# Packed attention with a routed feed-forward: copy of the turned pairs, order of the upper half and the route, start of batch 1

## Chip, cores and metric

One core of a Trainium2 chip runs the kernel. The metric is device time in microseconds (us) of one execution, lower is better. Engines are named as in the profile: PE (TensorE), DVE (VectorE), ACT (ScalarE), POOL (GpSimd), SP (SyncE, which issues DMAs).

## What is computed

Two stages on 8 batches. In the first, 32 pack queries `p` gather each head's keys and values, and the 576 queries attend to the 32 packed rows. In the second, each of the 4608 tokens goes through the one of eight experts whose embedding is nearest.

```python
def _attn_ref(q, k, v, p):                  # q, k, v: 8 x 8 x 576 x 64, p: 8 x 8 x 32 x 64
    p_packed = sm_attn(p, k, v)             # softmax(p k^T / 8) v
    return sm_attn(q, p_packed, p_packed)   # softmax(q pp^T / 8) pp

def _moe_ref(x, expert_emb, tau, w1, w2):   # x: 4608 x 512, w1: 8 x 512 x 1024
    logits = xn @ en.T / tau                # rows of x and emb divided by their norms
    expert_idx = np.argmax(logits, axis=1)
    gate_w = softmax(logits)[arange, expert_idx]
    for e in range(E):
        h = np.maximum(x[mask] @ w1[e], 0.0)
        out[mask] = gate_w[mask, None] * (h @ w2[e])
```

## The kernel before

The tokens of a batch mostly go to one expert. The kernel guesses it for the whole batch (`guess`), loads that expert's weights, runs the feed-forward of all 576 tokens with it, and counts afterwards how many tokens chose another; a loop behind the main one repeats a batch where there are any.

Most products are made of three passes, high by high, high by low and low by high: a value is cast on ACT to the high part and the rest is formed by a subtraction on DVE or POOL.

**What a batch's attention does, in order.** `att1`: the keys' scores (`key_scores`), their softmax; `pack`: the packed values land in one PSUM tile for two groups of heads (`values`); DVE multiplies them by the reciprocal sums and by masks, once for pairs of rows (`pair_rows`, tile `pp2`), once for four rows (`quad_rows`, L400, tile `pp`, 128x256, one instruction for each of two head groups); PE turns the pairs into the bank `pu` (`pair_turn`), a copy brings that into `T` (L496), and four products of `T` with the embeddings give the packed rows' logits (`row_logits`, L431). `rows_split` casts the four rows' products on ACT (L277) and subtracts on POOL (L278), into `ppx`. Then come the queries' scores against `T` (`query_scores`, L263, 16 products in two halves of 288 tokens) and the guess (L544 with a few small DVE steps, and a register load for the weights' DMAs).

`att2`: the softmax of the queries' scores in two halves, 0 and 1, each: transpose from PSUM (`unpack`, L586), `biggest` (L591), `shift` (L597), exponential on ACT (L600), `total` (L606), `norm` (L612), transpose back (`turn`, L621), and its split into `AT`: `high` a cast on ACT (L627), `low` a subtraction on DVE (L631). Then `route`: five tiles of up to 128 tokens. Each has six products of `AT` with `ppx` (L683), which give the logits' sums and the tokens' outputs; DVE reduces the logits (L692), and ACT squares the outputs with a running sum (L699) for the norm. Tiles 0 and 1 need half 0 of `AT` alone, the third tile (c = 2, tokens 256 to 383) is the first that needs half 1; its first products need the high part, the third the low. Two PSUM buffers `pt` hold the tiles: the third stands in the buffer of the first, the fourth in that of the second, and each is free when its reduction and its square are done. The square's output is of no use; it is written to a scratch tile with the tag `at`, of which there is one buffer, the same that the turned half lies in until `low` has read it.

Behind the route come the one-hot and the `counts` (L717, L727), and the `gates` (a chain of 128x5 steps, L106 to L111 and L744 onwards, a part of it on POOL in batch 0, then the spreading of the tail's gates, 16 small copies on ACT, L773).

**The feed-forward**, `ffn`: folding the packed values into the first weights (L836 to L850), 16 hidden products per half (L918, with a relu on ACT at L920 and the rest on DVE at L921), then the tail tokens, four tiles of 24 products of 320 columns (L946; `turn_tail`, L1266, transposes each tile on DVE while the next one's products run), then the output tiles, 24 products of 512 columns each (L964; the store's scaling at L1248).

**What sets the order.** Everything is issued in the order in which Python runs it. `ffn` yields after every few products; at each yield one step (sometimes two) of the next batch's attention is issued, so the attention of batch b+1 lies in batch b's feed-forward. `idle(n)` lets n such steps pass with nothing, and `alternate` takes one step of each of two generators by turns, the first named first. An engine executes its own instructions in that order and waits where an operand or a buffer isn't ready. For batch 0 a string, `PLAN`, says step by step what is issued beside the feed-forward: `a` is a step of batch 1's attention, `k` a flip of its queries, `r` a step of batch 0's route, `g` of its gates, `s` of its softmax. `tight` and `early` in the code mean batch 1, `first` and `fine` batch 0.

## Time and profile before

| | us |
|---|---|
| time, median of 3 runs | 460.75 (460.24 to 460.81) |
| the profiled execution | 461.09 |
| its span, first to last instruction | 459.5 |
| PE busy in the span | 430.4 (94%) |
| DVE / ACT / POOL busy | 316.0 / 217.8 / 148.2 |
| batch 2's feed-forward, start to start of batch 3's | 52.96 (148.30 to 201.26) |
| PE busy in it | 51.02 |
| PE busy between 56 and 70 (batch 0's feed-forward) | 10.13 of 14.00 |
| mean granted clock of PE | 0.993 of full speed |

The table's first half says that PE works nearly all the time and DVE two thirds of it. Batches 1 to 3 pass at the same pace, 52.94 to 52.96 each, so one of them stands for the middle of the run; the first one, in which batch 1's attention has to be started beside batch 0's, is different, and PE is idle there for almost 4 us in one stretch of 14. A share of busy time does not say who decides: for that one follows the waits and, from the end backwards, the chain of releases.

### The profile page before, as it was taken

Reading aid. Unit: us, or ns where it says so; the run is one execution under the profiler, and the core shown is the slowest. Engines: PE = TensorE matmul, PEld = TensorE weight load, DVE = VectorE, ACT = ScalarE, POOL = GpSimd, SP = SyncE. Lnnn points to the kernel's source line nnn. Section 1 sums busy time; section 2 is a strip of 40 time slices with the busy share of each in tenths; the row PEclk is TensorE's granted clock in tenths of the full one; section 3 lists DMA queues with packets and bytes.
Section 4 is the critical chain, followed back from the end, with each engine's and each line's share of the span. In section 5 each row is a group of like instructions: output and inputs, shape, how many; then the busy total and the mean of one; then the engine's idle time right before and its main releaser. Section 6 shows DMA issues by size and latency. Waiting matters only on the chain.

```text
span 459.5 us, 10722 instructions
## 1 busy us (share of the span) xinstructions
PE 430.4 (94%) x3890; PEld 364.9 (79%) x3891; DVE 316.0 (69%) x957; ACT 217.8 (47%) x580; POOL 148.2 (32%) x199
## 2 busy tenths in 40 slices
PE   8799979999999999999999999999999999899993
PEld 6547769788986979779887879869887888779993
DVE  5468869568974789648985689748895589535420
ACT  2456633675435733366443734357433754337300
POOL 2446564153403513053402524044221524026000
PEclk9999998999999999999999999999999999999998
DMA  7989899648995589854997479955798403621022
GB/s 208 293 271 260 232 262 316 181 97 212 300 317 130 133 228 328 235 123 124 255 350 174 100 211 304 296 110 134 234 359 209 108 3 122 245 57 47 3 59 51
DMA packets 48860, 88.23 MB, mean 192 GB/s; under 512 B 11992, under 2 KB 30488, under 8 KB 48800
## 3 DMA queue, kind: packets, MB, share of 16 engines
q1 hardware_dynamic: 40512, 57.96, 48.6%
q0 software_dynamic: 8000, 29.43, 18.0%
q8 instruction: 32, 0.52, 0.5%
q14 instruction: 28, 0.23, 0.2%
q10 hardware_dynamic: 288, 0.08, 0.1%
HBM read 78.00 MB, written 9.44 MB: 190 GB/s over the span
## 4 chain that ended last, share of the span: by engine, by line
PE 58%; DVE 27%; ACT 4%; DMA 4%; issue 3%; POOL 1%; SPq 1%; DVEq 0%; ACTq 0%; POOLq 0%
PE pf L964 19%; PE pf L918 17%; PE pf L946 5%; PE pt L683 4%; PE pt L836 3%; DVE hT L921 3%; DVE st L586 2%; PE pt L388 2%; DVE at L621 2%; DVE st L597 2%; PE pt L263 2%; DVE s L606 2%; DVE st L612 2%; DVE pp L400 2%; DVE mx L591 2%
## 5 line engine op out<-in xcount | busy, mean ns | idle before, releaser
L812 POOL TENSOR_TENSOR w2s<-w2r,w2s 128x512 fp32r<-128x512 f32 x61 | 78.5, 1292 | 168.9 <-ACT w2s L811 168.9
L946 PE MATMUL pf<-hT,w2s 128*128 128x320 f32 x768 | 124.3, 313 | 0.0
L946 PEld LDWEIGHTS pf<-hT,w2s 128*128 128x128 f32 x768 | 114.8, 190 | 3.7 <-issue 3.3
L918 PE MATMUL pf<-AT,G 128*128 128x288 f32 x720 | 103.7, 298 | 0.1
L918 PEld LDWEIGHTS pf<-AT,G 128*128 128x128 f32 x720 | 97.3, 188 | 4.7 <-issue 2.3
L964 PE MATMUL pf<-w2s,hT 128*128 128x512 f32 (+1 forms) x408 | 94.1, 383 | 0.0
L964 PEld LDWEIGHTS pf<-w2s,hT 128*128 128x128 f32 x408 | 72.0, 188 | 20.0 <-issue 5.9
L921 DVE SCALAR_TENSOR_TENSOR hT<-pf,hT 128x288 fp32r<-128x288 f32 x128 | 56.4, 446 | 20.2 <-ACT hT L920 20.2
L920 ACT ACTIVATE hT<-pf 128x288 fp32r<-128x288 f32 x128 | 51.4, 414 | 38.8 <-PE pf L918 37.5
L811 ACT CAST w2s<-w2r 128x512 fp32r<-128x512 f32 x64 | 39.0, 626 | 28.2 <-issue 26.4
L683 PE MATMUL pt<-ppx,AT 128*128 128x264 f32 (+1 forms) x240 | 38.3, 291 | 7.9 <-ACT at L699 6.8
L683 PEld LDWEIGHTS pt<-ppx,AT 128*128 128x128 f32 (+1 forms) x240 | 32.3, 177 | 12.5 <-ACT at L699 8.6
L850 DVE TENSOR_TENSOR G<-pt,G 128x512 fp32r<-128x512 f32 x28 | 19.4, 691 | 30.3 <-ACT G L849 30.3
L699 ACT ACTIVATE at<-pt 128x512 f32<-128x512 f32 (+1 forms) x40 | 23.9, 597 | 30.6 <-DVE lg L692 30.5
L278 POOL TENSOR_TENSOR ppx<-pp,ppx 128x256 fp32r<-128x256 f32 x16 | 11.4, 734 | 44.8 <-ACT ppx L277 44.8
L773 ACT COPY gt<-gate 32x2 f32<-32x2 f32 (+1 forms) x128 | 24.6, 192 | 2.2 <-DVE hit L1237 0.7
L600 ACT ACTIVATE st<-st 128x576 f32<-128x576 f32 (+1 forms) x17 | 11.2, 658 | 29.1 <-issue 19.5
L627 ACT CAST AT<-at 128x576 fp32r<-128x576 f32 x16 | 10.8, 673 | 27.8 <-DVE at L621 27.8
L849 ACT CAST G<-pt 128x512 fp32r<-128x512 f32 x28 | 16.5, 588 | 15.1 <-DVE G L850 12.0
L1266 DVE STREAM_TRANSPOSE ot<-pf 128x320 f32<-128x320 f32 x32 | 16.2, 506 | 9.9 <-PE pf L946 9.5
L293 DVE STREAM_TRANSPOSE kt<-nat 128x576 f32<-128x576 f32 x28 | 21.4, 764 | 0.1
L795 POOL DMA_DIRECT2D w2r<-in_moe_w x28 | 19.8, 713 | 0.0
(183 smaller groups left out, 491.8 us busy)
## 6 DMA issues: line engine op xcount, KB each, us to landing
nat<-in_k SPq DMA_DIRECT2D x112, 140.0 KB, 3.2
nat<-in_q SPq DMA_DIRECT2D x112, 140.0 KB, 3.8
w1t<-in_moe_w POOLq DMA_DIRECT2D x14, 1024.0 KB, 7.4
w2r<-in_moe_w POOLq DMA_DIRECT2D x28, 512.0 KB, 10.1
nat<-in_v SPq DMA_DIRECT2D x32, 160.0 KB, 3.8
out<-ot SPq DMA_DIRECT2D x28, 160.0 KB, 3.1
nat<-in_v SPq DMA_DIRECT2D x32, 128.0 KB, 4.0
out<-o SPq DMA_DIRECT2D x60, 64.0 KB, 1.7
```

Source lines behind the costliest of these rows:

```text
L293: nc.vector.transpose(kt.rearrange("p (n i) -> p n i", i=32), t)
L683: nc.tensor.matmul(pt[:r, 512 * g : 512 * g + XW], AT[:, a, g, c * P : c * P + r], x.ppx[:, m, g], start=(i == 0), stop=(i == 2),)
L699: nc.scalar.activation(scr[:r, :, : HB * D], ptv[:r, :, 0 : HB * D], AF.Square, accum_out=ss[:r, c : c + 1])
L773: copy(dst[32 * a : 32 * a + 32, k : k + HB * (n - 1) + 1 : HB], src[32 * k : 32 * k + 32, NCT : NCT + n],)
L795: queue.dma_start(t, w2e[:, 2 * i : 2 * i + 2, :])
L811: nc.scalar.copy(hi, raw)
L812: eng.tensor_tensor(out=lo, in0=raw, in1=hi.bitcast(F32), op=ALU.subtract)
L918: nc.tensor.matmul(pf[:, :HS], w, r, start=(n == 0), stop=(n == len(ops) - 1))
L920: nc.scalar.activation(hT[:, 0, f, cs], pf[:, :HS], AF.Relu)
L921: nc.vector.scalar_tensor_tensor(out=hT[:, 1, f, cs], in0=pf[:, :HS], scalar=0.0, in1=hT[:, 0, f, cs].bitcast(F32), op0=ALU.max, op1=ALU.s ...
L946: nc.tensor.matmul(pf[:, : S - TL], x.w2s[f][:, m, mt * P : mt * P + P], hT[:, a, f, TL:], start=(n == 0), stop=(n == len(ops) - 1),)
L964: nc.tensor.matmul(pf[:, :w], hT[:, a, f, c * P : (c + 1) * P], x.w2s[f][:, m, at : at + w], start=(f == 0 and i == 0), stop=(f == NF - 1 ...
```

## The change

It consists of these parts.

- In `pack`, for batches 2 to 7, the copy of `T` is issued ahead of the four rows' products. For batch 1 the copy moves from DVE to ACT.
- In `route`, the square's scratch tile takes the tag `st` (two buffers, those of the halves' scores) in place of `at`, but not in batch 0.
- In `softmax`, the cast and the subtraction of half 1 (`high(1)`, `low(1)`) are issued behind the first route tile's reduction and square. Three idle steps stand ahead of the route and two ahead of its second tile, and the alternation with the next keys begins with the keys.
- For batch 1 (`early`) both halves are unpacked first, the guess is issued ahead of the query scores, the query flips may start after the key scores, `shift` of half 1 is on DVE instead of POOL, and the rows of `PLAN` change to match; batch 0's route and counts come in other steps.

```diff
@@ -485,18 +485,20 @@
             if not tight:
                 yield
             pu = ps.tile([P, 512], F32, name="pu", tag="pf")
-            for g in range(NG):
-                quad_rows(x, g, pts[g])
             if tight:
+                for g in range(NG):
+                    quad_rows(x, g, pts[g])
                 yield
             for g in range(NG):
                 pair_turn(x, g, pu)
             if not tight:
                 yield
-            nc.vector.tensor_copy(x.T, pu[:, 0 : NG * P])
+            (nc.scalar.copy if tight else nc.vector.tensor_copy)(x.T, pu[:, 0 : NG * P])
             if tight:
                 yield
             else:
+                for g in range(NG):
+                    quad_rows(x, g, pts[g])
                 for g in range(NG):
                     rows_split(x, g)
                 yield from idle(2)
@@ -511,6 +513,8 @@
                 logits_split(x)
 
         key_scores(x)
+        if tight:
+            x.queries = queries()
         yield
         if tight:
             for g in range(NG):
@@ -520,7 +524,6 @@
                 key_exp(x, g)
                 key_sum(x, g)
                 yield
-            x.queries = queries()
             yield from pack()
             return
         for g in range(NG):
@@ -638,6 +641,8 @@
                 (unpack, 0), (biggest, 0), (shift, 0), (unpack, 1), (biggest, 1), (total, 0),
                 (shift, 1), (norm, 0), (turn, 0), (total, 1), (low, 0), (norm, 1), (turn, 1),
             )
+            if early:
+                order = (order[0], order[3], order[1], order[2], *order[4:])
             if first:
                 names = dict(
                     U=unpack, B=biggest, S=shift, X=expo, T=total, N=norm, R=turn, H=high, L=low
@@ -648,19 +653,23 @@
                 step(hf, *gs)
                 if step is shift and not first:
                     expo(hf)
-                if step is turn and not first:
+                if step is turn and not first and not hf:
                     high(hf)
                 yield
             if first:
                 return
-            yield
-            low(1)
             if not after:
+                high(1)
+                low(1)
                 return
-            yield
+            yield from idle(3)
             steps = route(x)
             yield next(steps)
-            yield from alternate(steps, after)
+            next(steps)
+            high(1)
+            low(1)
+            yield from idle(2)
+            yield from alternate(after, steps)
 
         yield from softmax()
 
@@ -673,6 +682,7 @@
         x.routed = lg, ss
 
     def route(x, fine=False):
+        scratch = dict(name="at", tag="at") if fine else dict(name="st", tag="st", bufs=2)
         AT = x.AT
         lg, ss = x.routed
         for c in range(NC5):
@@ -695,7 +705,7 @@
                 axis=AX.X,
                 op=ALU.add,
             )
-            scr = sb.tile([P, NG, HS], F32, name="at", tag="at")
+            scr = sb.tile([P, NG, HS], F32, **scratch)
             nc.scalar.activation(
                 scr[:r, :, : HB * D], ptv[:r, :, 0 : HB * D], AF.Square, accum_out=ss[:r, c : c + 1]
             )
@@ -1035,10 +1045,13 @@
                 counts(bat[b - 1])
             yield from att1(x, nat_main(b), b == 1)
             if b == 1:
+                expert = guess(x)
+                next(expert)
                 query_scores(x)
                 yield
-            expert = guess(x)
-            next(expert)
+            if b > 1:
+                expert = guess(x)
+                next(expert)
         second = att2(x, keys_main(b + 1) if b else None, b == 0, b == 1)
         if b == 1:
             drain(expert)
@@ -1301,13 +1314,13 @@
 
     PLAN = (
         "qssq", "sssssssss", "sss", "ss", "ss", "ssG", "", "sG", "ssa", "ssa",
-        "a", "sa", "a", "GG", "w", "aq", "aq", "a", "aq", "qw",
-        "aW", "wWa", "Wr", "wk", "rrak", "akw", "rka", "a", "a", "a",
-        "ra", "arr", "rra", "ra", "rra", "ra", "ga", "ga", "ga", "ga",
+        "a", "sa", "a", "GG", "w", "aq", "aq", "a", "aq", "qwk",
+        "aW", "wWa", "Wr", "wk", "rrak", "arkw", "a", "a", "a", "a",
+        "ra", "rra", "rra", "ra", "a", "a", "ga", "ga", "ga", "rrga",
         "ga", "a", "aag", "ga", "ga", "ga", "g", "g", "gaa", "a",
         "aa", "a", "a", "a", "g", "", "", "", "", "",
     )
-    POOLED = ("S1",)
+    POOLED = ()
     DBL = 8
     LAG = 2
```

DVE in batch 3's feed-forward, around the copy of `T` for batch 4 (`pp` are the four rows' products, `hT` the relu's rest, `rq_t` and `gy` steps of the gates). Before:

```order
L921 SCALAR_TENSOR_TENSOR hT<-pf,hT 128x288
L400 SCALAR_TENSOR_TENSOR pp_4017<-pt,ri,mask_77 128x256
L400 SCALAR_TENSOR_TENSOR pp_4019<-pt,ri,mask_77 128x256
L106 TENSOR_TENSOR rq_t<-rq_h,gy 128x5
L108 TENSOR_TENSOR rq_t<-rq_t,gy 128x5
L111 SCALAR_TENSOR_TENSOR gy<-rq_t,gy 128x5
L921 SCALAR_TENSOR_TENSOR hT<-pf,hT 128x288
L496 COPY T<-pu 128x256
L744 TENSOR_TENSOR gy<-gy,ss 128x5
```

After:

```order
L931 SCALAR_TENSOR_TENSOR hT<-pf,hT 128x288
L106 TENSOR_TENSOR rq_t<-rq_h,gy 128x5
L108 TENSOR_TENSOR rq_t<-rq_t,gy 128x5
L111 SCALAR_TENSOR_TENSOR gy<-rq_t,gy 128x5
L931 SCALAR_TENSOR_TENSOR hT<-pf,hT 128x288
L496 COPY T<-pu 128x256
L400 SCALAR_TENSOR_TENSOR pp_4032<-pt,ri,mask_77 128x256
L400 SCALAR_TENSOR_TENSOR pp_4034<-pt,ri,mask_77 128x256
L754 TENSOR_TENSOR gy<-gy,ss 128x5
```

The two products of four rows stood six instructions ahead of the copy; now they follow it directly, ahead of the same gate step. After them the second bank of the query scores, which lies in the PSUM buffer of the packed values, is also behind these products.

PE in the same feed-forward, from the guess (L544, now L547) over the five route tiles (L683, now L693) among tail products (L946, now L956) and output products (L964, now L974). Before:

```order
L544 MATMUL pu<-m_3320,itau 1x8 x2
L946 MATMUL pf<-hT,w2s 128x320 x60
L683 MATMUL pt<-ppx,AT 128x264 x6
L946 MATMUL pf<-hT,w2s 128x320 x4
L683 MATMUL pt<-ppx,AT 128x264 x6
L946 MATMUL pf<-hT,w2s 128x320 x8
L683 MATMUL pt<-ppx,AT 128x264 x6
L946 MATMUL pf<-hT,w2s 128x320 x8
L683 MATMUL pt<-ppx,AT 128x264 x6
L964 MATMUL pf<-w2s,hT 128x512 x6
L683 MATMUL pt<-ppx,AT 64x264 x6
L964 MATMUL pf<-w2s,hT 128x512 x21
```

After:

```order
L547 MATMUL pu<-m_3320,itau 1x8 x2
L956 MATMUL pf<-hT,w2s 128x320 x64
L693 MATMUL pt<-ppx,AT 128x264 x6
L956 MATMUL pf<-hT,w2s 128x320 x4
L693 MATMUL pt<-ppx,AT 128x264 x6
L956 MATMUL pf<-hT,w2s 128x320 x12
L693 MATMUL pt<-ppx,AT 128x264 x6
L974 MATMUL pf<-w2s,hT 128x512 x6
L693 MATMUL pt<-ppx,AT 128x264 x6
L974 MATMUL pf<-w2s,hT 128x512 x6
L693 MATMUL pt<-ppx,AT 64x264 x6
L974 MATMUL pf<-w2s,hT 128x512 x15
```

Four tail products moved ahead of the first tile, four more ahead of the third, and the fourth tile stands behind six output products.

DVE at the same place, from half 1's `norm` on (L612, now L615; L631, now L634, is `low`, L692, now L702, the reduction of a route tile, L1266, now L1279, a tail tile's transpose). Before:

```order
L612 TENSOR_TENSOR st<-st,s_4214 128x576
L621 STREAM_TRANSPOSE at<-st 128x576
L631 TENSOR_TENSOR AT<-at,AT 128x2x288
L692 TENSOR_REDUCE lg<-pt 128x8
L1266 STREAM_TRANSPOSE ot<-pf 128x10x32
L299 TENSOR_SCALAR pn<-pn 128x128
```

After:

```order
L615 TENSOR_TENSOR st<-st,s_4214 128x576
L624 STREAM_TRANSPOSE at<-st 128x576
L1279 STREAM_TRANSPOSE ot<-pf 128x10x32
L702 TENSOR_REDUCE lg<-pt 128x8
L634 TENSOR_TENSOR AT<-at,AT 128x2x288
L299 TENSOR_SCALAR pn<-pn 128x128
```

The tail tile's transpose and the reduction moved ahead of the low difference.

PE in batch 0's feed-forward, from the last route tile of batch 0 (64x264) over its counts (L727, L730; now L737, L740) to batch 1's own tiles. Before:

```order
L683 MATMUL pt<-ppx,AT 64x264 x6
L946 MATMUL pf<-hT,w2s 128x320 x8
L727 MATMUL pu<-oh,ones 1x32
L730 MATMUL pu<-oh,ones 1x8
L946 MATMUL pf<-hT,w2s 128x320 x32
L683 MATMUL pt<-ppx,AT 128x264 x6
L946 MATMUL pf<-hT,w2s 128x320 x4
L683 MATMUL pt<-ppx,AT 128x264 x6
L946 MATMUL pf<-hT,w2s 128x320 x8
L683 MATMUL pt<-ppx,AT 128x264 x6
```

After:

```order
L693 MATMUL pt<-ppx,AT 64x264 x6
L956 MATMUL pf<-hT,w2s 128x320 x28
L737 MATMUL pu<-oh,ones 1x32
L740 MATMUL pu<-oh,ones 1x8
L956 MATMUL pf<-hT,w2s 128x320 x16
L693 MATMUL pt<-ppx,AT 128x264 x6
L956 MATMUL pf<-hT,w2s 128x320 x4
L693 MATMUL pt<-ppx,AT 128x264 x6
L956 MATMUL pf<-hT,w2s 128x320 x4
L974 MATMUL pf<-w2s,hT 128x512 x9
```

The counts moved behind 20 more tail products, and between last tile and batch 1's first tile stand 44 products in place of 40.

## Rows read from the trace of the kernel before

**Rows 1.** Waits of PE: engine, line, waited for: us in total, times, longest.

```profile
PE pt L683 <- ACT at L699: 6.8, 7, 1.6
PE pu L431 <- DVE T L496: 5.9, 7, 1.0
PE pu L727 <- DVE oh L717: 2.3, 1, 2.3
...
PE pt L683 <- DVE lg L692: 1.0, 1, 1.0
```

**Rows 2.** Chain that ended last, 214 to 240: start us, us, instruction.

```profile
216.05 0.42 ACT hT L920
...
236.37 0.18 DVE lg L692
```

**Rows 3.** Timeline 212 to 225: start us, us, instruction [idle before <-releaser].

```profile
217.78 0.17 DVE L111 SCALAR_TENSOR_TENSOR gy<-rq_t,gy 128x5 f32<-128x5 f32 x1
...
218.23 0.87 DVE L400 SCALAR_TENSOR_TENSOR pp<-pt,ri,mask 128x256 f32<-128x256 f32 x2
...
218.79 0.74 ACT L277 CAST ppx<-pp 128x256 fp32r<-128x256 f32 x2 [0.73 <-DVE pp L400]
...
219.40 0.64 DVE L111 SCALAR_TENSOR_TENSOR gy<-rq_t,gy 128x5 f32<-128x5 f32 x1
...
220.33 0.41 DVE L496 COPY T<-pu 128x256 f32<-128x256 f32 x1
...
220.79 0.41 PE L431 MATMUL pu<-enT,T 128*64 128x8 f32 x8 [0.97 <-DVE T L496]
...
220.93 0.45 DVE L921 SCALAR_TENSOR_TENSOR hT<-pf,hT 128x288 fp32r<-128x288 f32 x1
```

**Rows 4.** Timeline 225 to 250, the route of batch 4.

```profile
232.71 1.18 PE L683 MATMUL pt<-ppx,AT 128*128 128x264 f32 x6
...
234.18 0.78 DVE L621 STREAM_TRANSPOSE at<-st 128x576 f32<-128x576 f32 x1
...
234.99 0.67 ACT L627 CAST AT<-at 128x576 fp32r<-128x576 f32 x1 [2.96 <-DVE at L621]
...
235.70 0.76 DVE L631 TENSOR_TENSOR AT<-at,AT 128x576 fp32r<-128x576 f32 x1 [0.74 <-ACT AT L627]
...
236.46 0.51 DVE L1266 STREAM_TRANSPOSE ot<-pf 128x320 f32<-128x320 f32 x1
236.63 0.60 ACT L699 ACTIVATE at<-pt 128x512 f32<-128x512 f32 x1 [0.97 <-DVE lg L692]
...
237.38 1.00 PE L683 MATMUL pt<-ppx,AT 128*128 128x264 f32 x6 [1.00 <-ACT at L699]
...
238.21 1.33 PE L946 MATMUL pf<-hT,w2s 128*128 128x320 f32 x8
...
239.38 0.89 PE L683 MATMUL pt<-ppx,AT 128*128 128x264 f32 x6
```

**Rows 5.** Timeline 68 to 84, batch 1's attention in batch 0's feed-forward.

```profile
68.20 1.03 DVE L717 TENSOR_TENSOR oh<-code,lmx 128x40 f32<-128x40 f32 x1
...
69.81 6.24 PE L946 MATMUL pf<-hT,w2s 128*128 128x320 f32 x31
...
73.64 0.69 DVE L631 TENSOR_TENSOR AT<-at,AT 128x576 fp32r<-128x576 f32 x1
...
76.56 0.83 POOL L745 TENSOR_SCALAR gy<-gy 128x5 f32<-128x5 f32 x1
...
80.84 2.43 ACT L773 COPY gt<-gate 32x3 f32<-32x3 f32 x12
```

**Rows 6.** Windows: busy us per engine, PEclk (granted clock), DMA share, GB/s.

```profile
71.50:72.50 1.00, 1.00 (x5) 1.00 (x5) 0.96 (x5) 0.00 (x0) 0.39 (x2) 0.50 1.10 294
```

**Rows 7.** A load of batch 1's queries: timeline; DMA issue, KB, us to landing.

```profile
43.25 1.45 SPq L178 DMA_DIRECT2D nat<-in_q  x1
...
nat<-in_q SPq DMA_DIRECT2D x1, 140.0 KB, 3.7
```


## The prediction

> **What bounds the kernel now.** I read the waits of TensorE first, then the chain of work that ended last, then the timeline of one batch (the feed-forward of batch 3, with the attention of batch 4 woven in) and that of batch 0's feed-forward, with the clock by stretches. TensorE is nearly always busy; of what it waits for, these matter here [rows 1]: seven times the third route tile waits for a square on ACT (6.8 us), seven times the four logit products wait for the copy of T (5.9), once the counts of batch 0 wait for the one-hot on DVE (2.3), once a route tile waits for a reduction (1.0).
>
> The waits look like 16 us to be had (6.8 + 5.9 + 2.3 + 1.0). The chain says that they aren't additive. In each middle batch it leaves TensorE at the relu of 216.05 and stays with DVE, with ACT between its steps, until the reduction at 236.37 [rows 2]; only then does TensorE carry it again. So DVE decides when the third route tile can run (237.38 [rows 4]), and a wait of TensorE ahead of that point is slack: filling it brings TensorE sooner to a wait that then grows. What a batch gains is how much work TensorE has done when the third tile is released, and how early it is released.
>
> **T ahead of the quads, batches 2 to 7.** Before, the copy at 220.33 stands behind two products of four rows (0.87) and a 128x5 step that took 0.64 where its like take 0.17, while POOL ran the two subtractions that follow the casts [rows 3]. Now both stand behind the copy: it ends 1.2 to 1.3 earlier, at about 219.5, and TensorE, ready at 220.79 - 0.97 = 219.82, doesn't wait. But the second bank of the query scores takes the buffer that the quads still read, so it waits for them: 219.5 + 0.87 = 220.35, where TensorE would be at 220.16. Of 0.97, 0.8 is recovered. The price is on DVE: on ACT the last relu (0.42 [rows 2]) still stands behind the two casts of the quads (0.74 for both), and these now come after the copy; quads to 220.3, the second cast to 220.65, relu to 221.07, so DVE's next product starts at 221.1 where it started at 220.93 [rows 3]. DVE's chain is 0.17 later.
>
> The lengthened step is the one unknown here. If POOL's subtractions (now from 220.3) lengthen another DVE step by 0.64 - 0.17 = 0.47, the chain is 0.6 late; if the stretch without it starts earlier, 0.2 early. I take 0.17, since DVE then waits for the relu anyway.
>
> The Trainium skill ("SBUF — State Buffer", section "Who interferes with whom") says that a DVE instruction with two SBUF inputs contends with a GpSimd instruction that reads SBUF, and that one blocks the other for its whole length. Its long 0.64 fits [rows 3]. By that rule the cost isn't removed but moved, to the two-input steps of the gates; the sum would then be 0.47 worse in each of six batches, 457.5 (454.7 + 2.8).
>
> **Third tile two items back, own buffer, upper half later.** On TensorE 64 tail products stand ahead of the first tile (60 before) and 12 between the second and the third (8). Eight such products take 239.38 - 238.21 = 1.17 [rows 4]. On DVE and ACT the upper half changes: before, transpose (ends 234.96), high cast, low difference, reduction of the first tile, then the square, which had to wait for the low difference since both use one buffer. Now: transpose, a turn of a tail tile (0.51), the reduction (0.17), the square (0.60), and behind it on ACT the high cast (0.67), then the low difference (0.76) [rows 4]. Each square still starts 0.1 after the reduction of its tile, own buffer or not (236.37 to 236.63, less the 0.17 of the reduction [rows 2, 4]), so the new buffer frees it of the low difference, not of DVE.
>
> Release: the transpose ends at 234.96 + 0.17 = 235.13, the turn at 235.6, the reduction at 235.75; the square starts at 235.85, the high cast at 236.45 and ends at 237.12; the low difference ends at 237.92. The third tile's first two products can start at 237.15, the third at 237.95; four more products end at 238.5.
>
> Arrival: TensorE stood ready for that tile at 237.38 - 1.00 = 236.38. The 0.8 and the four products ahead of the first tile (0.58) cancel nearly; that tile waits for its low half anyway (1.18 where an unhindered one takes 0.89 [rows 4]), which is 0.17 later. With four more products between: 236.38 + 0.17 + 0.58 = 237.13. So it arrives as the high half is ready and waits 0.5 inside the tile. Before, the same work (third tile plus eight products) was done at 239.38; now at 238.5. **Gain 0.88 a batch.** In batch 7 the same comparison gives 0.8 (five of 0.88 and one of 0.8 make 5.2). The fourth tile's buffer is free in time: its square needs the next reduction (238.5) and ends near 239.15, and six 512-column products lie ahead of the tile. Six batches: 5.2. Bounds for one batch: 0.4 with the 0.47 above, and 1.5 if the square could start with its tile, ahead of the reduction (then nothing waits at the third tile). The upper bound is far, since the reduction stands in DVE's queue; I take the value that my row-by-row sum gives.
>
> **Batch 1, in batch 0's feed-forward.** Unpacking both halves at once frees the buffer that the fourth tile of batch 0 waited for (1.0); the counts now stand 28 products behind the last tile instead of 8, which covers their 2.3. After that wait the granted clock was 0.50 (of 1.00; so 1.2 GHz), and 31 products took 6.24 [rows 5, 6], 0.20 each against 0.146: 1.7 more. Together 5.0. The shift of half 1 goes from POOL to DVE (0.7 for DVE, as the low difference of the same size [rows 5]), but DVE's last one-hot step, 1.03 while POOL did that shift [rows 5], should be short again, so DVE pays nothing net.
>
> Against that: the T copy, which on DVE followed the first tile's reduction directly, now stands on ACT behind that tile's square (0.60, and 0.1 to start): the logits come 0.7 to 1.0 later. But the query scores waited for the second square anyway, and the guess is now ahead of them: I leave 0.2 of it. First tile of batch 1: TensorE arrived at 75.9 (69.81 + 6.24, less the overlap), and now, 5.0 earlier, near 70.9. DVE's one-hot ended at 69.23; it should end 2.6 earlier, 1.4 as the last tile comes sooner and 1.2 by the short steps. The low half followed 5.1 later (74.33 [rows 5]); with the shift's 0.7 that is 5.8, so 72.5. So the tile waits 1.6 and comes 3.45 earlier than before, with four products fewer left (0.58): 4.0. The third tile then stands behind the gates: in DVE's order the reduction comes after the gate steps, and these need POOL's chain that ended at 77.39 [rows 5]; that starts some 2 us earlier, so high and low are ready near 78.4 and 79.2, and TensorE loses 2.1. The second square now stands behind all sixteen gate copies (twelve took 2.43 [rows 5]), so the fourth tile waits 1.2 more; the wait of the third tile before (0.2, the shortest of the seven) goes. 4.0 - 2.1 - 1.2 + 0.2: **0.9 left of 4.0.** Bounds: 4.5 without the last two waits; -1.4 if the first query flip, now ahead of the probabilities' copies on DVE, waits for its load, and the new waits bring the clock down once more (1.7). The load's last part was issued at 43.25 and landed 3.7 later, 46.95 [rows 7]; the flip's new place is at 46.7, so 0.25 as I read it, 1.4 if landing counts from the issue's end. I take 0.25; it is hidden by the T copy's wait.
>
> **Rivals.** *A, DVE swallows it:* the steady batches gain only 0.2: the lengthened step stays (0.47) and the third product starts another 0.2 later than I read it. For it: DVE has no gap from 217 to 236. Against: 1.17 of work was moved ahead and the release grows by less. 461.1 - 6 x 0.2 - 0.9 = 459.0. *B, batch 1 gives its gain back:* load and clock as bounded, -1.4: 461.1 - 5.2 + 1.4 = 457.3. For it: three new waits within 8 us; before, a 2.3 us wait behind shorter ones was enough for the clock to fall. *C, slower:* the high cast behind the first tile's square, in six batches. Transpose to third tile took 2.42 before; with 1.17 of work ahead it pays as long as it stays under 3.6, and my sum has 2.65 effective. If the turn, now ahead of the reduction, holds DVE until a late tail product, the release slips past 3.6; at 3.9 that costs 0.3 a batch and batch 1's stage gains nothing: 462.9. Against: the turn needs 72 products, and these end 2 us before. *D, more:* no wait in the third tile, 1.5 a batch and 3 in batch 1: 449.
>
> **How the numbers follow.** The profiled execution took 461.09, its span 459.5. 461.09 - 5.2 - 0.9 = 455.0; the median of the three runs, 460.75, lies 0.34 lower, so 454.7. Chances: forecast (451 to 457) 0.60, A 0.16, B 0.12, C 0.07, D 0.05. The forecast's ends are 0.6 and 1.2 a batch with batch 1 between 0 and 2.5. Leaving out C, most of D and the upper part of A, the range is 450.8 to 458.9. Faster by over 0.2% (0.9 us, about what a measurement here can tell from no change): the forecast, B, D and most of A, 0.89; within 0.2%: 0.04; slower: 0.07.
>
> **What would show it.** In the profile after: waits of the logit products for T gone except in batch 1, where ACT is named; the second bank of the query scores waiting about 0.2 for a quad; third tiles that start near their high cast and wait inside; the period of the middle batches at 52.1 where it was 52.96; no 2.3 before the counts and no half clock from 69 to 74. It would be wrong if the third tile's wait is over 1.5, if DVE's chain between relu and transpose grew by over 0.5, or if the stretch at half clock came back later.

## Result: 456.16 us, 1.1% faster

| | before | after |
|---|---|---|
| time, median of 4 runs, us | 460.78 (460.24 to 461.95) | 456.16 (455.04 to 456.87) |
| ratio, 95% interval | | 0.9894 (0.9866 to 0.9922) |
| profiled execution, us | 461.09 | 456.38 |
| batch 2's feed-forward, fold to fold, us | 52.94 | 52.00 |
| DVE busy, us | 316.0 | 313.4 |

The time lies within the range that was given (450.8 to 458.9), 1.5 above the forecast of 454.7. Whether the steps were right is a different question, and the time alone doesn't answer it. So both profiled executions are cut at the same instructions: the first hidden product (the first L918, now L928, at 38.38 and 37.53), the fold of batch 1's first weights (L836, now L846, at 88.14 and 87.38), the fold of batch 7's (407.21 and 400.59) and TensorE's last product (452.33 and 445.71).

| stretch | before | after | change | forecast |
|---|---|---|---|---|
| to the first hidden product | 38.38 | 37.53 | -0.85 | none |
| from there to batch 1's fold | 49.76 | 49.85 | +0.09 | -0.9 |
| six feed-forwards, batches 1 to 6 | 319.07 | 313.21 | -5.86 | -5.2 |
| last feed-forward to TensorE's end | 45.12 | 45.12 | 0.00 | none |
| from there to the end of the span | 7.17 | 9.09 | +1.92 | none |

The sum is -4.7, as the executions' difference. So the stage with six batches behaved as forecast, batch 1's gained nothing, and two stretches that the change doesn't touch moved by -0.85 and +1.92. The near agreement of the sum owes something to luck.

First the waits of TensorE after the change (engine, line, waited for: us in total, times, longest).

```profile
PE pt L693 <- DVE AT L634: 4.7, 14, 0.6
PE pt L388 <- DVE p1T L382: 1.5, 1, 1.5
PE pt L693 <- ACT AT L630: 1.2, 3, 0.6
...
PE pt L693 <- ACT st L709: 1.0, 1, 1.0
...
PE pu L431 <- ACT T L496: 0.9, 1, 0.9
```

Of [rows 1], the third tile's wait for a square (6.8), the logit products' for T on DVE (5.9), the counts' (2.3) and the reduction's (1.0) are gone; what is left at the route tiles (L693) is mostly a wait for the low half, twice a batch. A wait for the copies of the probabilities (L382) is new. The 0.2 that the query scores were to wait for the four rows' products isn't among the waits.

The timeline of batch 3's feed-forward after the change, at the places of [rows 3] (all 2.77 earlier: the relu that stands at 216.05 in [rows 2] starts at 213.28):

```profile
213.28 0.41 ACT L930 ACTIVATE hT<-pf 128x288 fp32r<-128x288 f32 x1 [2.25 <-PE pf L928]
...
216.30 0.41 DVE L496 COPY T<-pu 128x256 f32<-128x256 f32 x1
216.63 0.87 DVE L400 SCALAR_TENSOR_TENSOR pp<-pt,ri,mask 128x256 f32<-128x256 f32 x2
216.99 0.41 PE L431 MATMUL pu<-enT,T 128*64 128x8 f32 x8
217.19 0.74 ACT L277 CAST ppx<-pp 128x256 fp32r<-128x256 f32 x2 [1.90 <-DVE pp L400]
217.32 1.52 PE L263 MATMUL pt<-kt,T 64*32 64x288 f32 x32
...
217.67 1.43 POOL L278 TENSOR_TENSOR ppx<-pp,ppx 128x256 fp32r<-128x256 f32 x2 [8.01 <-ACT ppx L277]
218.28 0.46 DVE L931 SCALAR_TENSOR_TENSOR hT<-pf,hT 128x288 fp32r<-128x288 f32 x1 [0.51 <-ACT hT L930]
...
218.87 0.30 DVE L758 TENSOR_TENSOR lg<-lg,gy 128x40 f32<-128x40 f32 x1
```

The copy comes 1.26 earlier and TensorE doesn't wait for it. The price on DVE is there too: the next product waits 0.51 for the relu that stands behind the two casts, and starts at 218.28 + 2.77 = 221.05, where it started at 220.93.

And the route of batch 4, as in [rows 4]:

```profile
229.81 0.40 PE L693 MATMUL pt<-ppx,AT 128*128 128x264 f32 x2
...
230.59 0.76 PE L693 MATMUL pt<-ppx,AT 128*128 128x264 f32 x4 [0.38 <-DVE AT L634]
...
231.63 0.78 DVE L624 STREAM_TRANSPOSE at<-st 128x576 f32<-128x576 f32 x1
...
232.33 0.47 DVE L1279 STREAM_TRANSPOSE ot<-pf 128x320 f32<-128x320 f32 x1
...
232.73 0.14 DVE L702 TENSOR_REDUCE lg<-pt 128x8 f32<-128x16 f32 x1
232.96 0.60 ACT L709 ACTIVATE st<-pt 128x512 f32<-128x512 f32 x1 [3.47 <-DVE lg L702]
...
233.55 0.66 ACT L630 CAST AT<-at 128x576 fp32r<-128x576 f32 x1
234.25 0.76 DVE L634 TENSOR_TENSOR AT<-at,AT 128x576 fp32r<-128x576 f32 x1 [1.38 <-ACT AT L630]
234.26 0.51 PE L693 MATMUL pt<-ppx,AT 128*128 128x264 f32 x2
...
235.06 0.76 PE L693 MATMUL pt<-ppx,AT 128*128 128x264 f32 x4 [0.28 <-DVE AT L634]
```

With 2.77 added: square at 235.73 (forecast 235.85), high cast 236.32 (236.45), third tile 237.03 (237.15), its third product 237.83 (237.95), its end 238.43 (238.5, before 239.38).

### The profile page after: what moved, and what is told of

It reads as the page before. It is cut to its first block, busy times and chain, and to the rows that moved or that the text cites. A ratio compares the mean times of both kernels' runs of the same rounds, so it can differ in the third digit from the quotient of the medians.

```text
span 454.8 us, 10750 instructions
## 1 busy us (share of the span) xinstructions
PE 430.0 (95%) x3890; PEld 364.7 (80%) x3891; DVE 313.4 (69%) x957; ACT 217.1 (48%) x581; POOL 146.4 (32%) x198
## 4 chain that ended last, share of the span: by engine, by line
PE 57%; DVE 25%; ACT 6%; DMA 5%; issue 3%; POOL 1%; SPq 0%; DVEq 0%; POOLq 0%; ACTq 0%
PE pf L974 19%; PE pf L928 17%; PE pt L693 5%; PE pf L956 5%; DMA nat<-in_k 3%; PE pt L846 3%; DVE hT L931 3%; PE pt L388 2%; DVE st L589 2%; DVE s L609 2%; DVE AT L634 2%; DVE st L600 2%; PE pt L263 2%; PE pt L368 2%; DVE pp L400 1%
## 5 line engine op out<-in xcount | busy, mean ns | idle before, releaser
L956 PE MATMUL pf<-hT,w2s 128*128 128x320 f32 x768 | 121.8, 311 | 0.2 <-POOL w2s L822 0.2
L956 PEld LDWEIGHTS pf<-hT,w2s 128*128 128x128 f32 x768 | 113.3, 188 | 4.1 <-issue 3.3
L928 PE MATMUL pf<-AT,G 128*128 128x288 f32 x720 | 103.7, 298 | 0.1
L928 PEld LDWEIGHTS pf<-AT,G 128*128 128x128 f32 x720 | 97.3, 188 | 4.7 <-issue 2.3
L974 PE MATMUL pf<-w2s,hT 128*128 128x512 f32 (+1 forms) x408 | 95.2, 384 | 0.0
L974 PEld LDWEIGHTS pf<-w2s,hT 128*128 128x128 f32 x408 | 71.5, 188 | 19.4 <-issue 5.9
L693 PE MATMUL pt<-ppx,AT 128*128 128x264 f32 (+1 forms) x240 | 40.5, 295 | 7.4 <-DVE AT L634 4.7
L693 PEld LDWEIGHTS pt<-ppx,AT 128*128 128x128 f32 (+1 forms) x240 | 33.0, 177 | 14.0 <-DVE AT L634 7.7
L709 ACT ACTIVATE st<-pt 128x512 f32<-128x512 f32 (+1 forms) x35 | 20.9, 597 | 46.1 <-DVE lg L702 46.1
L278 POOL TENSOR_TENSOR ppx<-pp,ppx 128x256 fp32r<-128x256 f32 x16 | 11.5, 741 | 52.6 <-ACT ppx L277 52.6
L1279 DVE STREAM_TRANSPOSE ot<-pf 128x320 f32<-128x320 f32 x32 | 15.7, 491 | 9.2 <-PE pf L956 9.2
L1261 ACT ACTIVATE o<-pf,gate 128x512 f32<-128x512 f32 (+1 forms) x16 | 10.9, 679 | 16.6 <-issue 13.9
```

The source lines that it names most:

```text
L693: nc.tensor.matmul(pt[:r, 512 * g : 512 * g + XW], AT[:, a, g, c * P : c * P + r], x.ppx[:, m, g], start=(i == 0), stop=(i == 2),)
L709: nc.scalar.activation(scr[:r, :, : HB * D], ptv[:r, :, 0 : HB * D], AF.Square, accum_out=ss[:r, c : c + 1])
L928: nc.tensor.matmul(pf[:, :HS], w, r, start=(n == 0), stop=(n == len(ops) - 1))
L956: nc.tensor.matmul(pf[:, : S - TL], x.w2s[f][:, m, mt * P : mt * P + P], hT[:, a, f, TL:], start=(n == 0), stop=(n == len(ops) - 1),)
L974: nc.tensor.matmul(pf[:, :w], hT[:, a, f, c * P : (c + 1) * P], x.w2s[f][:, m, at : at + w], start=(f == 0 and i == 0), stop=(f == NF - 1 ...
```

## The experiments

Periods are the distance of two folds in the middle of the run, where those of one run lie within 0.06; times are medians (that of the kernel before was 460.96 to 461.52 on the chips of the experiments). The column to TensorE's end holds the distance between the folds of batches 1 and 2, which varies and is up to 1.3 longer than the period (below, at `no_b1`). The changed kernel was measured twice, `after` and `after_again`, and the two times differ by 1.2; so steps are priced by the periods and the stage, not by the last column.

| kernel | first hidden product to fold | period | first hidden product to TensorE's end | end stretch | time |
|---|---|---|---|---|---|
| before | 49.76 | 52.96 | 413.95 | 7.17 | 460.78 |
| after | 49.85 | 52.01 | 408.18 | 9.09 | 456.16 |
| `own_only` | 49.73 | 52.96 | 414.22 | 7.33 | 460.98 |
| `t_only` | 49.75 | 53.21 | 415.20 | 9.89 | 463.73 |
| `steps_only` | 49.84 | 52.20 | 409.54 | 7.16 | 455.89 |
| `no_late` | 49.85 | 52.43 | 410.68 | 7.76 | 457.57 |
| `no_t` | 49.82 | 51.78 | 406.88 | 7.36 | 453.89 |
| `no_b1` | 49.78 | 52.02 | 408.87 | 9.47 | 457.94 |
| `k_late` | 48.09 | 52.02 | 406.45 | 10.20 | 455.79 |
| `best` | 48.14 | 51.79 | 405.24 | 8.52 | 452.45 |
| `best_split` | 48.12 | 51.80 | 405.86 | 7.92 | 453.86 |
| `best_warm12` | 48.05 | 51.77 | 405.34 | 7.46 | 452.23 |
| `after_warm5` | 48.47 | 52.03 | 407.31 | 7.92 | 455.68 (one run) |
| `after_again` | 49.79 | 52.00 | 409.27 | 10.21 | 457.35 |

**The copy of T alone**, on the kernel before:

```diff
-            for g in range(NG):
-                quad_rows(x, g, pts[g])
             if tight:
+                for g in range(NG):
+                    quad_rows(x, g, pts[g])
                 yield
...
             else:
+                for g in range(NG):
+                    quad_rows(x, g, pts[g])
```

> The kernel before, with the copy of T ahead of the four rows' products in batches 2 to 7 and nothing else. My theory: the 0.7 that TensorE gains at the logit products is lost again at the third route tile, because the square that releases that tile is set by DVE's chain, which is 0.1 to 0.2 later; so the fold of the first weights comes every 52.96 to 53.15 us as before (52.96), the wait of the third tile for the square grows from 1.0 by 0.7 to 0.9, and the time is 460.8 to 461.8. Rival: the waits add up; then the period is 52.2 and the time 456.5.

Period 53.21, time ratio 1.0046 (1.0028 to 1.0065): slower. A step that takes 5.9 us of waiting off TensorE costs 0.25 a batch, a little over the 0 to 0.19 expected. The time is 2.3 above that of the kernel before, of which six batches explain 1.5 (6 x 0.25); the end stretch is long in this profile (9.89). The waits of TensorE in this kernel, where the third tile still waits for the square as much as in [rows 1], and the first tile now waits for the low half:

```profile
PE pt L685 <- ACT at L701: 6.8, 7, 1.6
PE pt L685 <- DVE AT L633: 3.2, 6, 0.5
```

One detail was otherwise than expected: the 0.7 was lost at the first tile, which reaches its low half too early, so the third tile's wait didn't grow.

**The copy of T put back**, in the changed kernel (the same edit backwards).

> The changed kernel with the copy of T back behind the four rows' products in batches 2 to 7. My theory, from the two timelines laid on each other: TensorE comes 0.7 later to the first route tile, but there it waited 0.4 for the low half, which is 0.2 earlier now; it reaches the third tile only 0.1 later, with the high and the low half 0.2 earlier; the tile ends 0.2 earlier than in the changed kernel. Period 51.8 (changed kernel 52.01), time 1.2 below the changed kernel's. Rival: the copy's 0.7 to 0.8 a batch is a real part of the 0.95 that a batch gained; then the period is 52.7 and the time 4 above.

Period 51.78, time ratio 0.9832 (0.9804 to 0.986): 2.3 faster than the changed kernel. In the two profiles 1.3 of that lies in the six batches (313.21 and 311.95); the rest is the end stretch, 1.7 shorter, less a first hidden product that starts 0.7 later. The timeline of its batch 3's feed-forward:

```profile
218.40 0.41 PE L431 MATMUL pu<-enT,T 128*64 128x8 f32 x8 [0.96 <-DVE T L496]
...
230.91 0.89 PE L691 MATMUL pt<-ppx,AT 128*128 128x264 f32 x6
...
234.70 1.26 PE L691 MATMUL pt<-ppx,AT 128*128 128x264 f32 x6
```

TensorE waits 0.96 for T again, and then hardly: the first tile takes its unhindered 0.89, the third finds its high half done and takes 1.26, with a short wait for the low half inside.

**The upper half put back**, in the changed kernel, batches 2 to 7:

```diff
-                if step is turn and not first and not hf:
+                if step is turn and not first and not (hf and early):
                     high(hf)
...
-            yield from idle(3)
+            if not early:
+                yield
+                low(1)
+            yield from idle(3 if early else 2)
...
-            high(1)
-            low(1)
+            if early:
+                high(1)
+                low(1)
```

> The changed kernel with the upper half's high cast and low difference back ahead of the first route tile's reduction (batches 2 to 7); the idle steps, the own buffer and the copy of T stay. My theory: the gain of a batch comes from the four tail products moved ahead of the third tile and the four ahead of the first, not from the late cast: DVE now does low difference, the tail tile's transpose and the reduction, the third tile starts about 0.6 later than in the changed kernel but doesn't wait inside, and ends 0.2 later: period 52.2. Rival: the late cast is what counts, since the square comes 1.7 later without it; then the period is 52.6 or more.

52.43, between the two: the theory's 52.2 was 0.2 short, and the rival's 52.6 not reached. The square stands behind the low difference and a tail tile's transpose (reduction at 235.14 in its timeline), and the third tile waits for it:

```profile
234.03 0.76 DVE L634 TENSOR_TENSOR AT<-at,AT 128x576 fp32r<-128x576 f32 x1 [0.74 <-ACT AT L630]
...
235.14 0.13 DVE L705 TENSOR_REDUCE lg<-pt 128x8 f32<-128x16 f32 x1
...
235.37 0.60 ACT L712 ACTIVATE st<-pt 128x512 f32<-128x512 f32 x1 [1.37 <-DVE lg L705]
...
236.11 1.00 PE L696 MATMUL pt<-ppx,AT 128*128 128x264 f32 x6 [0.79 <-ACT st L712]
```

**The squares' buffer alone**, on the kernel before, and **the moved steps without T and the late half**:

```diff
+        scratch = dict(name="at", tag="at") if fine else dict(name="st", tag="st", bufs=2)
-            scr = sb.tile([P, NG, HS], F32, name="at", tag="at")
+            scr = sb.tile([P, NG, HS], F32, **scratch)
```

> The kernel before, with the squares of batches 1 to 7 written to their own buffer and nothing else. My theory: the square starts 0.1 after its tile's reduction on DVE in either case, and that reduction stands behind the low difference in DVE's order, so nothing moves: folds 52.96 apart as before, third tile's wait 1.0. Rival: the buffer was what the square waited for; then the square starts with its tile, about 1 earlier, and the period is 52.2 or less.

52.96, ratio 0.9997 (0.9983 to 1.0012): nothing.

> The changed kernel with both the copy of T and the upper half's cast and difference of batches 2 to 7 back at their old places: of what was done to these batches, the idle steps ahead of the route and of its third tile are left, and the squares' own buffer. My theory: the third tile is released 0.2 earlier than with T ahead (52.43), since DVE is 0.2 earlier: period 52.2. With the run that has only T put back (51.78), the moved products are then worth 0.75 of a batch's 1.18, the late upper half 0.4. Rival: the late half needs T ahead, and here nothing changes: 52.4.

52.20. (Of the idle steps, the two stand ahead of the route's third tile, not of its second: `next(steps)` in the diff issues the second.) With it the period splits without a remainder: the moved products, with the order of the alternation, -0.76 (52.96 to 52.20), the late upper half -0.42 (52.20 to 51.78), the early T +0.23 (51.78 to 52.01; without the late half 52.20 to 52.43, on the kernel before 52.96 to 53.21), the buffer 0.00. That the late half works without the own buffer wasn't tried: the square would be queued on ACT ahead of the cast whose reader has to free its buffer.

**Batch 1 as before**, batches 2 to 7 as changed (the parts marked `tight` and `early`, the guess's place, `POOLED` and `PLAN` as in the kernel before):

```diff
-            (nc.scalar.copy if tight else nc.vector.tensor_copy)(x.T, pu[:, 0 : NG * P])
+            nc.vector.tensor_copy(x.T, pu[:, 0 : NG * P])
...
-            if early:
-                order = (order[0], order[3], order[1], order[2], *order[4:])
...
-    POOLED = ()
+    POOLED = ("S1",)
```

> The changed kernel with all that concerns batch 1 undone (its plan, guess, unpacking, copy of T, shift, own buffer and late upper half); batches 2 to 7 as changed. My theory, from the stages: between the first hidden product and the first fold the change as a whole brought -0.1 (49.76 before, 49.85 after), since the waits that it took away there came back as others; so this kernel needs 49.7 to 49.9 there, the later folds are 52.01 apart, and the time is that of the changed kernel within 1. Rival: the batch 1 part brought the 0.8 by which the first fold came earlier; then the fold is at 88.1 and the time 0.8 higher.

49.78 to the fold: all that the change does for batch 1 moves its own stage by less than 0.1. The time is 1.8 above the changed kernel's first measurement, not within 1, and 0.6 above its second. In the profile 0.7 lies between batch 1's fold and batch 2's (52.82 against 52.08), which no other kernel's edit explains either: that distance is up to 1.3 above the period of the same run, while the later ones agree. In `after_again` (53.28) its timeline names the load of batch 2's values:

```profile
109.03 0.90 PE L388 MATMUL pt<-nat,p1T 128*32 128x64 f32 x40 [1.16 <-DMA nat<-in_v]
```

**The first flip of batch 1's queries one step later:**

```diff
-        "a", "sa", "a", "GG", "w", "aq", "aq", "a", "aq", "qwk",
-        "aW", "wWa", "Wr", "wk", "rrak", "arkw", "a", "a", "a", "a",
+        "a", "sa", "a", "GG", "w", "aq", "aq", "a", "aq", "qw",
+        "aWk", "wWa", "Wr", "wk", "rrak", "arkw", "a", "a", "a", "a",
```

> The changed kernel with the first flip of batch 1's queries one step later in batch 0's plan, behind the copies of the probabilities. In the changed kernel DVE waited 1.5 at this flip for the load, and the value products 1.5 for the copies behind it. My theory: both waits go, DVE is busy without a gap from there to the copy of T, so nearly all arrives at the first fold: it starts at 86.0 to 86.4 (87.38 in the changed kernel, 88.14 before), and the time falls by 1.0 to 1.4. Rival: later waits of batch 1's route swallow it; the fold starts at 87.2 or later.

48.09, 1.76 less than the changed kernel and more than the theory's 1.0 to 1.4; the fold at 85.54. In the changed kernel's timeline DVE stood at the flip, and TensorE's value products behind the copies that follow it:

```profile
47.38 0.78 DVE L293 STREAM_TRANSPOSE kt<-nat 128x576 f32<-128x576 f32 x1 [1.51 <-DMA nat<-in_q]
...
48.75 1.73 PE L388 MATMUL pt<-nat,p1T 128*32 128x64 f32 x80 [1.48 <-DVE p1T L382]
```

With the flip behind those copies both waits are gone from the timeline:

```profile
47.28 1.73 PE L388 MATMUL pt<-nat,p1T 128*32 128x64 f32 x80
...
48.55 0.76 DVE L293 STREAM_TRANSPOSE kt<-nat 128x576 f32<-128x576 f32 x1
```

The waits are not the whole gain (below, at batch 1). The time fell by 0.4 only; the end stretch of this kernel takes 10.2, where the changed kernel's took 9.1.

**T back and the flip later together.**

> The changed kernel with the copy of T back behind the four rows' products (batches 2 to 7) and the first flip of batch 1's queries one step later: the two earlier runs in one. My theory: the two gains lie in different stages and add up: folds 51.78 apart (changed kernel 52.01), first hidden product to first fold 48.1 (changed kernel 49.85), and from the first hidden product to TensorE's end 405.2 (408.18). What follows TensorE's end was 7.2 to 10.2 in the six kernels so far, so the time is 451.5 to 455.5. Rival: the flip's gain is worth less without the early copy of T, in batch 2; then 406 or more to TensorE's end.

Both gains add up: 405.24 to TensorE's end. Time 452.45, ratio 0.9811 (0.9779 to 0.9843): faster than the kernel before and than the changed one.

**The end stretch.** It was 7.2 to 10.2 in kernels that share all code there. SP issues four stores for each of the last half tiles. Those of the first half in the changed kernel's timeline of SP (start us, us, instruction):

```profile
443.45 0.33 SPq L1272 DMA_DIRECT2D out<-o  x1
443.82 1.20 SPq L1272 DMA_DIRECT2D out<-o  x1
445.06 1.67 SPq L1272 DMA_DIRECT2D out<-o  x1
446.78 0.43 SPq L1272 DMA_DIRECT2D out<-o  x1
```

The second and the third of the same four in the timeline of the kernel before:

```profile
450.44 0.43 SPq L1259 DMA_DIRECT2D out<-o  x1
450.92 0.43 SPq L1259 DMA_DIRECT2D out<-o  x1
```

The DMA queue that loads instructions has a packet at 443.7 and one at 445.1 after the change. Four experiments bear on it, the first with the stores split:

```diff
-                nc.sync.dma_start(rs, t)
+                (nc.scalar if w < DM and a % 2 else nc.sync).dma_start(rs, t)
```

> The same, with the stores of the last output tile issued by SP and ACT by turns instead of SP alone. In the six kernels so far the stretch from TensorE's end to the end was 7.2 to 7.8 where two loads of instructions fell near TensorE's end, and 9.1 to 10.2 where a third fell 2.0 to 2.25 ahead of it; in those, single store issues of SP took 1.0 to 2.0 instead of 0.43. My theory: SP's own queue of issues sets that stretch; with half of them on ACT it is 6.3 to 6.6 with two loads, and at most 8 with three. Rival: the landing of the last store sets it, whoever issues; then it stays at 7.2 or more.

7.92, neither as expected: there was no third load, yet SP waited 4.3 in two waits for stores that ACT had issued to land, so the split made a wait of its own and tells nothing of the queue. SP's waits (us in total, times, longest):

```profile
SPq L1270 <- DMA out<-o: 4.3, 2, 2.5
```

The changed kernel with a shorter warm-up:

```diff
-    WARM = (13, 0)
+    WARM = (5, 0)
```

> The changed kernel with 5 warm-up products at its start instead of 13, so that TensorE's code is shorter by 32 instructions (nothing else reads them). My theory: the third load of instructions near TensorE's end is one of its own code, at a fixed place in it; with everything 32 instructions earlier it falls behind TensorE's end or into the jump there, SP's store issues take 0.43 again, and the stretch from TensorE's end to the end is 7.2 to 7.8 (changed kernel 9.09). Rival: the load belongs to another engine or to the moment; then it stays near -2.0 and the stretch is 9 or more. The first 40 us may differ, with fewer warm-up products.

Two loads, each of the last eight store issues at 0.6 or less, 7.92. One profile, but as forecast.

> The changed kernel once more. My theory: that a third load of instructions falls close ahead of TensorE's end, and that SP's store issues take over 1 there, belongs to this program and not to the one execution: the stretch behind TensorE's end is 8.5 to 10 again. Rival: chance; then it is 7.2 to 7.8 in this profile. Folds 52.01 apart, time 455 to 457 in either case, and the first hidden product at 37.4 to 38.4, which I take for a matter of when the first weights land.

Three loads again, 10.21, single issues of 1.28, 1.67 and 1.73; the time, 457.35, is a little above the 455 to 457 expected. And `best` with `WARM = (12, 0)`:

> The changed kernel with the copy of T back and the first flip one step later, and with 12 warm-up products instead of 13, so that TensorE's code is 4 instructions shorter ahead of all else. In the two runs of one program the third load of instructions near TensorE's end came both times, so I take it to hang on the program; whether 4 instructions are enough to lose it I can't say. My theory: load and long store issues go together, whatever the count: with two loads near the end every store issue of SP takes 0.7 or less and the stretch behind TensorE's end is 7.2 to 7.9, time 450.5 to 452; with three, some take over 1 and it is 8.5 to 10.2, time 452 to 454. From the first hidden product to TensorE's end 405.2 to 405.9, folds 51.79 apart. Rival: the two have nothing to do with each other; then there are long issues with two loads, or none with three.

Two loads, none of the last eight issues over 0.43, 7.46, time 452.23, 0.2 above the range expected (ratio 0.9816, 0.9791 to 0.9842): the same as `best` within the intervals.

## Why the prediction came out as it did

**That waits aren't additive** was right and is what the runs show best. `t_only` removes 5.9 of waiting and is slower.

**T ahead of the quads.** Its price was put at 0.17 a batch on DVE, with 0.2 early and 0.6 late as ends; by the runs it is 0.23. What the sum got wrong is the other side: it booked 0.8 of recovered waiting against the four products ahead of the first tile as if one paid for the other. The sum of the batch came out right (0.88 forecast, 0.95 measured), but T's share of it is negative. The same numbers would have shown it: the first tile needs the low half, which TensorE reaches too early either way, so TensorE's earlier arrival is worth nothing there, and DVE's 0.2 is lost.

The lengthened step of [rows 3] (0.64) has no successor of that size. While POOL's two subtractions run (from 217.67 on), DVE waits 0.51 for the relu and has one product with two inputs in SBUF, L758, which takes 0.30 where it took 0.20; so 0.1 is left of the 0.47. The Trainium skill ("SBUF — State Buffer", section "Who interferes with whom") says that a DVE instruction with two SBUF inputs contends with a GpSimd instruction that reads SBUF, and calls the ports that they share an exclusive lock. The trace agrees: L758 ends at 219.17, just behind POOL's second subtraction (219.11), as the 0.64 step ended at 220.04 beside one that ended at 220.03. The 2.8 worked out by that rule didn't come, since L758 started 0.24 ahead of POOL's end and nothing of the kind met the rest.

**Third tile, own buffer, late half.** Right to 0.13 at each of its five points; the buffer is worth nothing by itself, as said.

**Batch 1** is the step that failed: 0.9 forecast, -0.1 measured. What was to go, went: the counts' 2.3, the reduction's 1.0 and the half clock (windows of 70 to 74; the columns are those of [rows 6]). Before:

```profile
70.00:74.00 4.00, 4.00 (x19) 4.00 (x18) 3.86 (x12) 0.67 (x1) 1.48 (x7) 0.57 1.03 281
```

After:

```profile
70.00:74.00 4.00, 3.18 (x21) 2.71 (x20) 3.90 (x11) 1.14 (x2) 2.18 (x8) 1.00 1.04 304
```

The granted clock is 1.00 after the change, though TensorE idles in that stretch. Of what came back, the flip was mis-sized: 0.25, hidden, where DVE waited 1.51. The value taken came from a misreading of [rows 7]: each flip waits for four loads, and the one issued at 43.25 is the third. The fourth, in the kernel before (issue; KB, us to landing):

```profile
44.77 0.62 SPq L178 DMA_DIRECT2D nat<-in_q  x1
...
nat<-in_q SPq DMA_DIRECT2D x1, 140.0 KB, 2.7
```

It landed at 47.50, not at 46.95. After the change it was issued at 42.36, 2.4 earlier, and landed at 47.30, only 0.2 earlier, while DVE was ready for the flip at 45.87, not at 46.7, with the first hidden product 0.85 earlier. So the upper bound of 1.4 was met by luck: its condition was that landing counts from the issue's end, and the third load landed at 46.91, as counted from the start. (The stage's lower bound of -1.4 doesn't follow from the two prices beside it either: 0.9 - 1.4 - 1.7 is -2.2.)

And the wait isn't the whole loss. Behind the flip and the copies DVE has two products `w2s` with two inputs in SBUF, then the four rows' products. After the change the second of them stands beside a subtraction of POOL:

```profile
50.30 1.29 POOL L822 TENSOR_TENSOR w2s<-w2r,w2s 128x512 fp32r<-128x512 f32 x1 [0.44 <-ACT w2s L821]
50.51 1.63 DVE L822 TENSOR_TENSOR w2s<-w2r,w2s 128x512 fp32r<-128x512 f32 x1
```

In `k_late` the same product comes late beside the subtraction ahead of that one:

```profile
49.59 0.74 DVE L822 TENSOR_TENSOR w2s<-w2r,w2s 128x512 fp32r<-128x512 f32 x1
```

In all fourteen profiles this product ends 0.54 to 0.56 behind the end of the subtraction of POOL that it stands beside; alone, the next one in `k_late` takes 0.68. In the kernel before and in `k_late` it is POOL's earlier subtraction, after the change the next, and the four rows' products start 12.8 and 14.5 behind the first hidden product: the 1.7 by which the changed kernel's stage is longer than that of `k_late`. TensorE pays it in two waits, for the copies and, at a route tile of batch 0, for the four rows' products (1.48 and 0.42; in `after_again` 0.88 and 1.03). So the loss is a step and doesn't grow with the wait. In the five profiles with the changed plan in which the flip waits 0.92 to 1.51, the stage takes 49.79 to 49.85; in `after_warm5`, with the same plan, the flip waits 0.48, the product falls to POOL's earlier subtraction, and the stage takes 48.47. The prediction had no such term. No run changes POOL's subtraction alone: that it holds DVE's product is read from these ends.

T on ACT makes TensorE wait 0.88 (0.17 before), where 0.2 was left of it. The others were forecast too dear (1.6, 2.1 and 1.2 for the first, third and fourth tile; the trace has 0.82, 0.85 and 1.03):

```profile
72.53 0.51 PE L693 MATMUL pt<-ppx,AT 128*128 128x264 f32 x2 [0.26 <-ACT AT L630]
73.60 0.76 PE L693 MATMUL pt<-ppx,AT 128*128 128x264 f32 x4 [0.56 <-DVE AT L634]
...
78.94 0.51 PE L693 MATMUL pt<-ppx,AT 128*128 128x264 f32 x2 [0.57 <-ACT AT L630]
79.73 0.76 PE L693 MATMUL pt<-ppx,AT 128*128 128x264 f32 x4 [0.28 <-DVE AT L634]
...
82.92 1.00 PE L693 MATMUL pt<-ppx,AT 128*128 128x264 f32 x6 [1.03 <-ACT st L709]
```

So rival B held by half: the early flip took the gain, by the load's wait and POOL's subtraction together, and the clock didn't fall again. With the flip one step later the stage gains 1.7 (`k_late`).

**The stretches outside** weren't in the sum. The first hidden product starts between 37.24 and 38.87 in the fourteen profiles, with the same code ahead of it but for the warm-up; the kernel before waits there 0.6 for the first weights' load, the changed one doesn't, but `best`, the earliest of all, waits 0.5. What sets it stays open. The end stretch is below.

**Among the cases**, the profiled execution, 456.38, lies between the forecast (455.0 by the same sum) and B (457.3), nearer to B. By its parts it is 0.7 better than the forecast in the six batches, 1.0 worse in batch 1 (-0.1 between 0.9 and B's -1.4, in part for a reason that B hadn't), and 1.1 worse in stretches that no case had. That these parts cancel to within 1.4 is luck.

## What to carry over

Before filling a wait of the engine that looks bound, ask at which later place it meets the chain that decides, and what filling it adds to that chain; here the longest-looking wait but one was slack and cost 0.23 a batch to remove. Work moved ahead of the place where two chains meet is the gain, and a step moved ahead in time must be checked against loads, which keep their own time, and for what it pushes back on its own engine: here 0.9 of waiting or 1.5 cost the same 1.7, since a product behind it fell beside another engine's work. And cut both profiles at the same instructions before crediting a change with its sum: two stretches that it didn't touch moved by -0.85 and +1.92.

## What the runs showed of the hardware

Of fourteen profiles, eight have 32 loads of instructions and six have 33 (the page's rows on DMA queues, before and after):

```profile
q8 instruction: 32, 0.52, 0.5%
```

```profile
q8 instruction: 33, 0.54, 0.5%
```

That is 16 KB each. They come at nearly the same counts of TensorE's instructions in every kernel, so I take them for its code; the Trainium skill ("Runtime: NRT & Kernel Launch", section "Instruction fetch mechanics") has each engine fetch its code in 16 KiB blocks, and calls the cost mostly hidden. At one place here long issues go with a load: in the six with 33 an extra one falls 2.5 to 0.5 ahead of TensorE's end, some of SP's last eight store issues take 1.0 to 2.0 instead of 0.43, and the end stretch is 8.5 to 10.2; in the eight with 32 none of the last eight takes over 0.7 and it is 7.2 to 7.9. Both programs whose warm-up was shortened (by 32 and by 4 instructions) lost the load and the long issues together, and the changed kernel had them in both its profiles. What decides whether the extra load comes isn't settled: `t_only`, with 7881 TensorE instructions in its trace, has it, `no_t`, with 7882, doesn't. Nor is it whether the load holds SP up or both answer to something else.
